# Sparse attention and two dense layers on one core: attention laid out as five-step jobs in issue order, weight conversion cut into three parts

## The chip, the cores and the metric

One NeuronCore of a Trainium2 chip runs the whole program in one launch. The metric is the device time in microseconds (us) of an execution; less is better. Engines by their names in the profile: PE is the matrix engine (TensorE), PEld its weight loads, DVE the vector engine, ACT the scalar engine, POOL the GpSimd engine, SP the queue that issues DMA transfers.

## The reference, cut to what matters

```
scores = (q @ k.T) / 8                     # 4 batches x 8 heads, 576 tokens, head size 64
scores = where(scores >= max(scores) - tau, scores, -1e9)
attn   = exp(scores - max) / (sum + 1e-9)
x  = (attn @ v), heads side by side         # 2304 tokens x 512
h  = x @ w_in;    x = moe_act(h) @ w_out    # 512 -> 2048 -> 512, (h+1)^2/4 between -1 and 1
h  = x @ w_in2;   y = (h * clip(h+3, 0, 6) / 6) @ w_out2
```

## The kernel before

**Attention** is 16 jobs, each one batch and a pair of heads; a job is five blocks of query rows (four of 128, and the last 64 rows of both heads together). So there are 80 steps, and step t stands for block t % 5 of job t // 5. For a step, `em_scores` makes the scores of two heads by eight PE records into two pairs of PSUM banks (P0, P1), DVE negates them into `p` and takes the row extreme `nm` (line 296), ACT takes the exponential `e` (line 300), DVE adds tau into `th` (line 303) and masks, multiplies and sums (line 306). The result `p` is then turned (transposed on PE, line 244): four 128-column pieces a head by `em_pt`, which ACT copies to `Gf` (line 327), and the last 64 columns of both heads by `em_tail`, which ACT copies to `Gt` (line 341). `pv_chunk` multiplies by v (line 361). Once a job `unit_q` and `unit_k` turn the next q and k, `pre_norm` and `em_norm` divide by the sums and write to memory (`xd`).

**Weights** of the dense layers come as 64-bit words; each 128x512 tile (an item) is converted into a pair hi, lo: two ACT operations (lines 111 and 114), a clamp (POOL line 115 during the attention), two DVE operations (lines 122 and 128), a POOL add (line 130), hi (POOL line 133, or ACT line 135 once dense work has begun), lo (POOL line 137). `split_a` and `split_b` are the two halves; 20 items are needed by the first dense pass.

**The first dense pass** (`dense1`: `em_h`, line 485, and `em_part`, line 542; 256 tokens at a time, the first 10 of 16 tiles of the hidden layer) begins when the first batch (four jobs) is done and is laid between the pieces of the attention by a credit: each `yield` of the attention adds `share`, and three matmuls of 128x256 (here called a unit) take 0.33. There are 480 units in all. What is left of it, and the rest of the dense layers, follows the attention.

**Order.** A scheduler with a simulated timeline sets the order of the instructions on each engine, except where `after(...)` puts one instruction behind another on the same engine (`pe_pins`).

Of the kernel before, what the change touches and what calls it, by code (L numbers as in the profile page):

```python
# [18 lines left out]
def kernel(  # L19
# [13 lines left out]
    V, S, G, T = nc.vector, nc.scalar, nc.gpsimd, nc.tensor  # L33
# [52 lines left out]
    def load_w(kind, m, f):  # L86
        t = stage.tile([128, 512, 2], U32, tag="w_raw", name="w_raw", bufs=RAW)
        if kind == "i":
            src = w_bits[m][0][:, f * 256:(f + 1) * 256].rearrange("(k p) n -> p k n", p=128)
            nc.sync.dma_start(out=t.rearrange("p (k n) r -> p k (n r)", k=KD), in_=src)  # L90
        else:
            src = w_bits[m][1][f * 128:(f + 1) * 128, :]
            nc.sync.dma_start(out=t.rearrange("p n r -> p (n r)"), in_=src)
        wraw[kind, m, f] = t

    def after(ins, prev):
        if prev is not None:
            tc.add_manual_dep(ins.ins, prev.ins.name, mybir.DependencyInfo(
                mybir.DependencyClass.NoSync, mybir.DependencyReason.DATA), reason="pace")

    pe_pins = []
    pins = {"S": None, "V": None, "G": None}

    def split_a(kind, m, f):
# [7 lines left out]
        after(x, pins["S"])  # L112
        if mode["att"]:
            S.activation(out=f32(c), in_=f32(t[:, :, 1]), func=ACTF.Abs)
            G.tensor_scalar(
                out=f32(c), in0=f32(c), scalar1=122879.9921875, scalar2=2.0 ** -15, op0=ALU.min, op1=ALU.max)
        else:
            S.activation(out=f32(c), in_=f32(t[:, :, 1]), func=ACTF.Abs)
            x = V.tensor_scalar(
                out=f32(c), in0=f32(c), scalar1=2.0 ** -15, scalar2=122879.9921875, op0=ALU.max, op1=ALU.min)  # L120
            after(x, pins["V"])
        V.tensor_scalar(out=c, in0=c, scalar1=3, scalar2=0x3FFFFFFF,  # L122
                        op0=ALU.logical_shift_left, op1=ALU.bitwise_and)
        wc[kind, m, f] = (hi, lo, c, t, r)

    def split_b(kind, m, f):
        hi, lo, c, t, r = wc.pop((kind, m, f))
# [3 lines left out]
        after(x, pins["G"])  # L131
        if mode["att"] and not mode["mlp"]:
# [10 lines left out]
    class Weights:  # L143


        def __init__(self):
# [3 lines left out]
            self.mid = False  # L150
# [9 lines left out]
        def half(self):  # L160
            if self.done < len(self.items):
                it = self.items[self.done]
                if not self.mid:
                    self.prefetch()
                    split_a(*it)
                else:
                    split_b(*it)
                    self.done += 1
                    self.prefetch()
                self.mid = not self.mid  # L170

        def one(self):
            n = self.done
            while self.done == n and n < len(self.items):
                self.half()

        def upto(self, n):
            while self.done < min(n, len(self.items)):
                self.half()
# [20 lines left out]
    mode = {"mlp": False, "att": True, "step": False, "t": 0, "s": 0, "n": 0}  # L200
# [4 lines left out]
    qt, kt = {}, {}  # L205
# [4 lines left out]
    def load_q(j):  # L210
# [3 lines left out]
        for h in HEADS:  # L214
            src = q[b, 2 * hp + h]
            nc.sync.dma_start(out=qn[:, 0:4, h * D:(h + 1) * D], in_=rows(src))
            nc.sync.dma_start(out=qn[0:TAIL, 4, h * D:(h + 1) * D], in_=src[MAIN:SEQ, :])

    def load_k(j):
# [3 lines left out]
        for h in HEADS:  # L223
            src = k[b, 2 * hp + h]
            nc.sync.dma_start(out=kn[:, 0:4, h * D:(h + 1) * D], in_=rows(src))
            for r in range(2):
                nc.sync.dma_start(out=kn[r * TAIL:(r + 1) * TAIL, 4, h * D:(h + 1) * D], in_=src[MAIN:SEQ, :])

    def load_v(j):
# [4 lines left out]
        for h in HEADS:  # L234
            src = v[b, 2 * hp + h]
            nc.sync.dma_start(out=t[:, 0:4, h, :], in_=rows(src))
            nc.sync.dma_start(out=t[h * TAIL:(h + 1) * TAIL, 4, h, :], in_=src[MAIN:SEQ, :])
# [5 lines left out]
    def turn(out, in_, pin):  # L243
        x = T.transpose(out, in_, ident)  # L244
        if pin:
            pe_pins.append(x)

    def unit_q(j):
# [3 lines left out]
        for c in range(5):  # L252
            turn(tm[:, c * 128:(c + 1) * 128], qn[:, c, :], c == 0)
        load_q(j + 1)
# [3 lines left out]
    def unit_k(j):  # L258
# [4 lines left out]
        for i, c in enumerate((4, 0, 1, 2, 3, 4)):  # L263
            turn(tm[:, i * 128:(i + 1) * 128], kn[:, c, :], i == 0)
        load_k(j + 1)
# [5 lines left out]
    def em_scores(j, i):  # L271

        last = i == NBLK - 1
# [4 lines left out]
        prev = None  # L278
        c = slice(i * 128, i * 128 + (TAIL if last else 128))
        for x, (h, e) in enumerate(((0, 0), (1, 1), (0, 1), (1, 0)) if last else ((0, 0), (1, 0), (0, 1), (1, 1))):  # L280
# [541 lines left out]
```

## Time and profile before

| | |
|---|---|
| median of three runs | 1201.52 us (1201.37 to 1201.78) |
| the profiled execution | 1200.08 us, of which 1198.3 us from the first to the last instruction (the span) |
| PE / DVE / ACT / POOL busy in the span | 1138.7 / 579.6 / 627.5 / 418.8 us |

PE is called busy from the start of a matmul to its modelled end, and matmuls overlap, so that a busy PE is not one at its peak. The stages are read from a table of stretches (rows below) and not from these totals.

### The profile page before, as it was taken

The page shows a single profiled execution, that of the slowest core. Times are in us where ns is not written, and L with a number is a line of the kernel's source. Part 1 is how long each engine was busy: PE and PEld are TensorE (multiplying, and loading weights), DVE is VectorE, ACT ScalarE, POOL GpSimd, SP SyncE. Part 2 cuts the span into 40 slices and gives each one's busy share as a digit, 9 for nine tenths or more (in the row PEclk, how much of TensorE's full clock was granted, in tenths as well). Part 3 has the DMA queues.
Part 4 walks back from the last instruction along what each step waited for, and adds up shares of the span by engine and source line. Part 5 has one row for each costly group of instructions (what it writes and reads, how often), then busy time and mean ns, then how long its engine had stood idle before and what let it go on. Part 6 is the DMA issues. An engine that isn't in the chain of part 4 may idle for free.

```text
span 1198.3 us, 17942 instructions
## 1 busy us (share of the span) xinstructions
PE 1138.7 (95%) x6656; PEld 906.7 (76%) x6656; DVE 579.6 (48%) x1196; ACT 627.5 (52%) x1217; POOL 418.8 (35%) x397
## 2 busy tenths in 40 slices
PE   4877799998999999999999999999999999999998
PEld 3444477876777787777888988888888888888886
DVE  3899865456555565553652575555740121121111
ACT  4667766565665665664665676654542222233222
POOL 1767531110111111112673666656742213222221
PEclk9999889999999999999999999999999999999999
DMA  4444421212111222003431244453210010010000
GB/s 114 117 133 135 128 81 30 51 50 59 54 35 31 59 59 68 21 20 107 149 103 47 81 136 150 152 168 98 88 43 15 1 58 9 1 44 2 18 1 35
DMA packets 106791, 82.43 MB, mean 69 GB/s; under 512 B 66512, under 2 KB 90576, under 8 KB 106704
## 3 DMA queue, kind: packets, MB, share of 16 engines
q1 hardware_dynamic: 106704, 81.29, 23.0%
q8 instruction: 52, 0.85, 0.3%
q14 instruction: 35, 0.29, 0.1%
HBM read 63.96 MB, written 17.30 MB: 68 GB/s over the span
## 4 chain that ended last, share of the span: by engine, by line
PE 83%; DVE 6%; ACT 4%; DMA 3%; SPq 2%; issue 2%; POOL 0%; ACTq 0%; DVEq 0%
PE Q L485 33%; PE P L527 26%; PE Q L542 7%; PE Q L361 6%; PE P L284 5%; PE Q L244 5%; DVE p L306 2%; DVE p L296 2%; DMA w_raw<-in_moe_w_in_dram 1%; PE P L244 1%; ACT e L300 1%; DMA w_raw<-in_moe_w_out_dram 1%; DVE w_c L122 1%; ACT r L494 1%; DVE w_c L128 1%
## 5 line engine op out<-in xcount | busy, mean ns | idle before, releaser
L503 POOL TENSOR_TENSOR gl<-r,gh 128x512 fp32r<-128x512 f32 (+1 forms) x190 | 205.9, 1084 | 641.7 <-ACT gh L502 624.1
L485 PE MATMUL Q<-xh,wih 128*128 128x512 f32 (+1 forms) x760 | 264.5, 349 | 0.7 <-ACT xh L468 0.5
L485 PE MATMUL Q<-xl,wih 128*128 128x512 f32 (+1 forms) x760 | 257.8, 339 | 0.2 <-DVE xl L469 0.2
L485 PE MATMUL Q<-xh,wil 128*128 128x512 f32 (+1 forms) x760 | 257.6, 339 | 0.0
L499 DVE SCALAR_TENSOR_TENSOR r<-r,Q 128x512 f32<-128x512 f32 (+1 forms) x80 | 50.7, 633 | 248.9 <-ACT r L498 248.8
L485 PEld LDWEIGHTS Q<-xh,wih 128*128 128x128 f32 x760 | 144.7, 191 | 29.9 <-issue 10.6
L502 ACT ACTIVATE gh<-r 128x512 fp32r<-128x512 f32 (+1 forms) x190 | 99.9, 526 | 121.5 <-PE P L527 53.3
L485 PEld LDWEIGHTS Q<-xl,wih 128*128 128x128 f32 x760 | 144.8, 191 | 16.5 <-DVE xl L469 0.7
L485 PEld LDWEIGHTS Q<-xh,wil 128*128 128x128 f32 x760 | 144.6, 190 | 15.6 <-issue 0.5
L296 DVE TENSOR_SCALAR_CACHE_REDUCE p<-P 128x576 f32<-128x576 f32 x144 | 104.1, 753 | 80.0 <-PE Q L244 71.5
L306 DVE SCALAR_TENSOR_TENSOR p<-p,th,e 128x576 f32<-128x576 f32 x144 | 130.9, 923 | 24.0 <-ACT e L300 17.4
L244 PE MATMUL Q<-ident,p 128*128 128x128 f32 (+1 forms) x656 | 113.8, 287 | 21.1 <-DVE p L306 10.1
L300 ACT ACTIVATE e<-p,nm 128x576 f32<-128x576 f32 x144 | 109.8, 773 | 32.7 <-DVE p L296 31.6
L498 ACT ACTIVATE r<-Q,three 128x512 f32<-128x512 f32 (+1 forms) x80 | 51.4, 643 | 143.4 <-PE Q L485 140.3
L244 PEld LDWEIGHTS Q<-ident,p 128*128 128x128 f32 (+1 forms) x656 | 74.6, 143 | 63.0 <-DVE p L306 11.7
L284 PE MATMUL P<-kt,qt 64*128 64x288 f32 (+1 forms) x640 | 109.1, 450 | 13.7 <-DVE p L296 7.5
L496 DVE SCALAR_TENSOR_TENSOR r<-r,Q 128x256 f32<-128x256 f32 (+1 forms) x110 | 55.0, 500 | 131.9 <-ACT r L495 129.5
L527 PE MATMUL P<-woh,gh 128*128 128x512 f32 x288 | 111.9, 390 | 0.6 <-DVE ob L580 0.6
L527 PE MATMUL P<-wol,gh 128*128 128x512 f32 x288 | 112.2, 390 | 0.0
L527 PE MATMUL P<-woh,gl 128*128 128x512 f32 x288 | 110.9, 390 | 0.0
L130 POOL TENSOR_TENSOR w_c<-w_c,w_raw 128x512 int32<-128x512 int32 x64 | 87.4, 1366 | 39.3 <-DVE w_c L128 28.1
L327 ACT ACTIVATE Gf<-Q 128x512 f32<-128x512 f32 x128 | 75.0, 591 | 48.6 <-PE Q L244 48.5
(81 smaller groups left out, 1865.2 us busy)
## 6 DMA issues: line engine op xcount, KB each, us to landing
w_raw<-in_moe_w_in_dram SPq DMA_DIRECT2D x32, 512.0 KB, 3.8
w_raw<-in_moe_w_out_dram SPq DMA_DIRECT2D x32, 512.0 KB, 3.6
xst<-xd SPq DMA_DIRECT2D x28, 256.0 KB, 3.2
kn<-in_k_dram SPq DMA_DIRECT2D x32, 128.0 KB, 2.6
qn<-in_q_dram SPq DMA_DIRECT2D x32, 128.0 KB, 2.6
vn<-in_v_dram SPq DMA_DIRECT2D x32, 128.0 KB, 2.6
xd<-xu SPq DMA_DIRECT2D x16, 256.0 KB, 2.5
x2d<-ob SPq DMA_DIRECT2D x16, 256.0 KB, 3.4
```

The costliest lines, as they stand in the source:

```text
L130: x = G.tensor_tensor(out=c.bitcast(I32), in0=c.bitcast(I32), in1=r, op=ALU.add)
L244: x = T.transpose(out, in_, ident)
L284: mm = T.matmul(o, qt[j][r, c], kt[j][r, k0:k0 + HS], start=True, stop=True, skip_group_check=True)
L296: V.tensor_scalar(out=p[:, x], in0=s[:, :, 0:HS], scalar1=-1.0, scalar2=3e38, op0=ALU.mult, op1=ALU.min, accum_out=nm[:, x:x + 1])
L300: S.activation(out=e, in_=p[:, x], func=ACTF.Exp, bias=nm[:, x:x + 1], scale=-1.0)
L306: V.scalar_tensor_tensor(out=p[:, x], in0=p[:, x], scalar=th[:, x:x + 1], in1=e, op0=ALU.is_le, op1=ALU.mult, accum_out=zt[j][:, z:z + 1])
L327: S.activation(out=f[:, h, :, d0:d0 + 128], in_=tm.rearrange("p (c n) -> p c n", c=4), func=ACTF.Copy)
L485: mm = T.matmul(h, l[:, kk * 128:(kk + 1) * 128], r, start=(x == 0), stop=(x == 3 * KD - 1))
L502: x = S.activation(out=gh, in_=r, func=ACTF.Copy)
L503: y = G.tensor_tensor(out=gl, in0=r, in1=f32(gh), op=ALU.subtract)
L527: T.matmul(a, l, r, start=(first and x == 0), stop=(last and x == 2))
L542: mm = T.matmul(o, l, r, start=(f == 0 and x == 0 and i == 0), stop=(f == NF1 - 1 and x == 2 and i == 1), skip_group_check=True)
```

## The change: what it does

- `Chain` wraps all five engines. While the attention runs, each instruction is put behind the one that was issued before it on its engine, so that the order there is the order of the code.
- A step is written as five pieces, with a place for dense work after each: (1) scores of t, the turned tail of t-2 in spare columns of a score bank, the row extremes, the exponentials of t, the masks of t-1; (2) the first turned half of t-2, and q or k of the next job; (3) normalization; (4) a part of the product with v of the job before; (5) the second turned half of t-2. Before, turns stood one step behind the scores (the tail two).
- `th` goes from DVE to POOL, the copy of the tail from ACT to DVE.
- A weight item is converted in three parts. Before dense work begins, one part a step (before: one half a step, and one more every third step); from then on two parts a step, and what `ahead1` demands at once.
- The credit is 0.22 a piece until the 20 items are converted, then 0.53 (before: 0.57).
- q, k and v of later jobs are loaded a step later (`later`), x for the dense pass earlier (`load_x`), tau first of all.

```diff
+    class Chain:
+        def __getattr__(self, name):
+            fn = getattr(self.engine, name)
+            def issue(*a, **k):
+                x = fn(*a, **k)
+                if mode["att"]:
+                    after(x, self.last)
+                    self.last = x
+                return x
+            return issue
+    V, S, G, T, Q = (Chain(e) for e in (nc.vector, nc.scalar, nc.gpsimd, nc.tensor, nc.sync))
...
+                (split_1, split_2, split_3)[self.stage](*it)
+                self.stage = (self.stage + 1) % 3
...
-        tl = bank("Q0" if mode["mlp"] else "Q3")
-            S.activation(out=t[:, d0:d0 + 128], in_=tl[:, 0:128], func=ACTF.Copy)
+        tl = s[:, 1, 320:448]
+            V.tensor_copy(out=gt_[:, d0:d0 + 128], in_=tl)
...
-        V.tensor_scalar(out=th[:, 0:n], in0=nm[:, 0:n], scalar1=taus[:, 0:1], scalar2=None, op0=ALU.add)
+        G.tensor_scalar(out=th[:, 0:n], in0=nm[:, 0:n], scalar1=taus[:, 0:1], scalar2=None, op0=ALU.add)
...
+        for t in range(n + NBLK):
             mode["t"] += 1
             mode["step"] = True
+            j, i = divmod(t, NBLK)
+            due, later[:] = later[:], []
+            ss = em_scores(t) if t < n else [unit_bank()]
+            if 0 <= t - 2 < n:
+                em_tail(t - 2, ss[-1])
+            if t < n:
+                em_first(t, ss)
+            if 0 <= t - 2 < n:
+                em_tail_copy(t - 2, ss[-1])
+            if t < n:
+                em_exp(t)
+            if 0 <= t - 1 < n:
+                em_mask(t - 1)
             yield
+            copy = em_pt(t - 2, 0) if 0 <= t - 2 < n else None
+            if i == 1:
+                unit_q(j + 1)
+            if i == 2:
+                unit_k(j + 1)
+            if copy:
+                copy()
+            yield
+            if i == 1 and j:
                 pre_norm(j - 1)
+            if i == 4 and j:
                 em_norm(j - 1)
                 done_jobs.add(j - 1)
+            yield
+            if j and i < 4:
+                em_pv(j - 1, "aabb"[i], ((0, 1, 2), (3, 4))[i % 2])
+            yield
+            if 0 <= t - 2 < n and order[t - 2][1] < NBLK - 1:
+                em_pt(t - 2, 1)()
+            for fn, x in due:
+                fn(x)
+            yield
...
+                if (g, 0) not in loaded_x:
+                    load_x(g)
+                    for _ in range(8 if mode["att"] else 0):
+                        yield None
...
-            if mode["t"] >= 3 and mode["step"]:
+            if mode["t"] >= 4 and mode["step"]:
                 mode["step"] = False
-                weights.half()
-                if mode["t"] % 3 == 0:
-                    weights.half()
+                weights.third()
...
-        credit = min(credit + share, 3.0)
+        piece += 1
+        if piece % 5 in (0, 2) and weights.done < 2 * NF1:
+            weights.third()
+        credit = min(credit + shares[weights.done == 2 * NF1], 3.0)
```

In the rows of order below, those of the changed kernel all carry line 44, the line in `Chain` that issues them. First DVE before dense work begins, before the change, at the second job (a number behind `P` is one of the score buffers):

```order
L296 TENSOR_SCALAR p,nm<-P_481 128x576
L296 TENSOR_SCALAR p,nm<-P_482 128x576
L122 TENSOR_SCALAR w_c<-w_c 128x512
L303 TENSOR_SCALAR th<-nm,taus 128x2
L128 SCALAR_TENSOR_TENSOR w_c<-w_raw,w_c 128x512
L306 SCALAR_TENSOR_TENSOR p,z<-p,th,e 128x576
```

The same engine and place in the changed kernel:

```order
L44 TENSOR_SCALAR p,nm<-P_429 128x576
L44 TENSOR_SCALAR p,nm<-P_430 128x576
L44 COPY Gt<-P_430 128x128
L44 SCALAR_TENSOR_TENSOR p,z<-p,th,e 128x576 x2
L44 TENSOR_SCALAR w_c<-w_c 128x512
L44 SCALAR_TENSOR_TENSOR w_c<-w_raw,w_c 128x512
```

The masks (`p,z<-p,th,e`) that stand behind the row extremes of a step are now those of the step before, `th` has left the engine, the tail copy has come, and the two weight operations stand behind the masks, once in three steps.

Second, ACT of the changed kernel in step 36, where dense work and conversion run side by side and `ahead1` demands two items at once:

```order
L44 ACTIVATE e<-p,nm 128x576
L44 ACTIVATE Gf<-Q_2035 128x4x128
L44 ACTIVATE w_raw<-w_raw 128x512
L44 ACTIVATE w_c<-w_raw 128x512
L44 ACTIVATE woh_2041<-w_c 128x512
L44 ACTIVATE w_raw<-w_raw 128x512
L44 ACTIVATE w_c<-w_raw 128x512
L44 ACTIVATE woh_2068<-w_c 128x512
L44 ACTIVATE Gf<-Q_2085 128x4x128
```

Each `woh` needs the POOL add of its own item, which comes after the second row above it; the second `Gf` copy of the attention stands behind both. Before, these rows stood apart, as here during the second job:

```order
L111 ACTIVATE w_raw<-w_raw 128x512
L300 ACTIVATE e<-p,nm 128x576
L327 ACTIVATE Gf<-Q_464 128x4x128
L300 ACTIVATE e<-p,nm 128x576
L114 ACTIVATE w_c<-w_raw 128x512
L367 ACTIVATE xu<-Q_455 128x320
```

Third, PE of the changed kernel late in the attention, from the end of a step's product with v into the next step:

```order
L44 MATMUL Q_5127<-xh,wil_552 128x256
L44 MATMUL Q_5155<-ident,p 128x128 x4
L44 MATMUL Q_5071<-gh,woh_1757 128x256
L44 MATMUL Q_5071<-gl,woh_1757 128x256
L44 MATMUL Q_5071<-gh,wol_1758 128x256
L44 MATMUL P_5164<-kt,qt 128x288
L44 MATMUL P_5165<-kt,qt 128x288
L44 MATMUL P_5164<-kt,qt 128x288
L44 MATMUL P_5165<-kt,qt 128x288
L44 MATMUL P_5165<-ident,p 128x128
```

The first row ends a tile of the hidden layer (`em_h`); the next rows are the second turned half, one unit of `em_part`, the scores and the tail. From step 40 on, every step holds eight units, and the end of `em_h` stands in its fourth or fifth piece, right ahead of or behind that turned half. By the order, the changed kernel has laid 0 units ahead of the scores of step 26, 54 ahead of step 40 and 368 ahead of step 79.

## Rows read from the trace of the kernel before

**Rows 1.** Busy time by stretches (us from the span's start).

```profile
core 0: us, PE busy (x) PEld busy (x) DVE busy (x) ACT busy (x) POOL busy (x), PEclk, DMA share, GB/s
33.40:146.30 112.90, 86.63 (x545) 51.72 (x543) 101.93 (x219) 78.43 (x156) 74.97 (x73) 0.92 0.45 126
296.00:536.00 240.00, 236.67 (x1768) 182.71 (x1766) 135.38 (x372) 148.24 (x319) 33.47 (x49) 1.00 0.16 44
700.00:1198.30 498.30, 493.45 (x2275) 411.52 (x2273) 162.66 (x226) 195.15 (x329) 192.13 (x153) 1.00 0.19 59
```

**Rows 2.** Timeline of PE: scores of step 3, q in steps 3 and 23, scores of step 79.

```profile
22.40 1.24 PE L284 MATMUL P<-kt,qt 64*128 64x288 f32 x8 [0.53 <-DVE p L296]
33.37 0.76 PE L244 MATMUL P<-ident,qn 128*128 128x128 f32 x5
146.29 0.77 PE L244 MATMUL P<-ident,qn 128*128 128x128 f32 x5
529.71 1.19 PE L284 MATMUL P<-kt,qt 64*64 64x288 f32 x8
```

**Rows 3.** Timeline of DVE: the first weight item; `pre_norm` in steps 45 and 80.

```profile
26.36 0.43 DVE L122 TENSOR_SCALAR w_c<-w_c 128x512 uint32<-128x512 uint32 x1 [3.75 <-POOL w_c L115]
295.86 0.57 DVE L378 TENSOR_SCALAR z<-z 128x9 f32<-128x9 f32 x1
535.90 0.17 DVE L378 TENSOR_SCALAR z<-z 128x9 f32<-128x9 f32 x1
```

**Rows 4.** Groups of instructions in 33.4 to 146.3 us: busy, mean ns | idle before.

```profile
L306 DVE SCALAR_TENSOR_TENSOR p<-p,th,e 128x576 f32<-128x576 f32 x36 | 42.2, 1188 | 6.7 <-ACT e L300 5.6
L128 DVE SCALAR_TENSOR_TENSOR w_c<-w_raw,w_c 128x512 uint32<-128x512 uint32 x18 | 12.6, 702 | 0.2
L122 DVE TENSOR_SCALAR w_c<-w_c 128x512 uint32<-128x512 uint32 x17 | 12.5, 733 | 1.2 <-POOL w_c L115 1.2
L303 DVE TENSOR_SCALAR th<-nm,taus 128x2 f32<-128x2 f32 x15 | 5.6, 371 | 0.3
L341 ACT ACTIVATE Gt<-Q 128x128 f32<-128x128 f32 x16 | 4.4, 274 | 0.0
L111 ACT ACTIVATE w_raw<-w_raw 128x512 int32<-128x512 uint32 x18 | 12.3, 682 | 12.8 <-DMA w_raw<-in_moe_w_in_dram 8.9 <-DMA w_raw<-in_moe_w_out_dram 3.9
L130 POOL TENSOR_TENSOR w_c<-w_c,w_raw 128x512 int32<-128x512 int32 x17 | 23.6, 1390 | 24.0 <-DVE w_c L128 21.5 <-DVE z L378 2.5
L115 POOL TENSOR_SCALAR w_c<-w_c 128x512 f32<-128x512 f32 x18 | 13.1, 728 | 8.4 <-ACT w_c L114 7.5
```

**Rows 5.** Groups of instructions in 296 to 536 us.

```profile
L485 PE MATMUL Q<-xh,wih 128*128 128x256 f32 x140 | 44.3, 316 | 0.2 <-DVE r L496 0.2
L542 PE MATMUL Q<-gh,woh 128*128 128x256 f32 x132 | 41.8, 317 | 0.0
L306 DVE SCALAR_TENSOR_TENSOR p<-p,th,e 128x576 f32<-128x576 f32 x63 | 51.5, 832 | 8.8 <-ACT e L300 5.3
L496 DVE SCALAR_TENSOR_TENSOR r<-r,Q 128x256 f32<-128x256 f32 x34 | 14.2, 418 | 25.5 <-ACT r L495 25.2
```

**Rows 6.** Timeline of PE: the first and the last of nine dense matmuls in a row.

```profile
226.78 0.28 PE L542 MATMUL Q<-gh,woh 128*128 128x256 f32 x1
...
227.73 0.28 PE L542 MATMUL Q<-gh,wol 128*128 128x256 f32 x1
```

**Rows 7.** Longest wait of PEld in 296 to 536 us: us, times, longest.

```profile
PEld Q L485 <- issue: 6.9, 16, 0.5
```

**Rows 8.** PE groups of the first pass: two rows before 529.7 us, two in 554 to 600 us.

```profile
L485 PE MATMUL Q<-xh,wih 128*128 128x256 f32 x220 | 70.1, 319 | 0.2 <-DVE r L496 0.2
L542 PE MATMUL Q<-gh,woh 128*128 128x256 f32 x195 | 62.1, 318 | 0.1
...
L542 PE MATMUL Q<-gh,woh 128*128 128x256 f32 x27 | 7.7, 285 | 0.1
L485 PE MATMUL Q<-xh,wih 128*128 128x256 f32 x4 | 1.1, 283 | 0.0
```

More of the change, by code (lines that the diff above doesn't have):

```diff
@@ L149, in __init__ @@
             self.done = 0
[L150 removed]
+            self.stage = 0
         def add(self, m, fs):
@@ L158, in prefetch, with third, half @@
                 self.loaded += 1
-        def half(self):
+        def third(self):
             if self.done < len(self.items):
                 it = self.items[self.done]
-                if not self.mid:
+                if self.stage == 0:
                     self.prefetch()
-                    split_a(*it)
-                else:
-                    split_b(*it)
+                (split_1, split_2, split_3)[self.stage](*it)
+                self.stage = (self.stage + 1) % 3
+                if self.stage == 0:
                     self.done += 1
                     self.prefetch()
[L170 to L175, printed above, removed]
+        def half(self):
+            if self.stage == 0:
+                self.third()
+                self.third()
+            else:
+                while self.stage and self.done < len(self.items):
+                    self.third()
         def upto(self, n):
             while self.done < min(n, len(self.items)):
-                self.half()
+                self.third()
     weights = Weights()
@@ L353, in pv_chunk, with em_pv @@
+        return copy
+    o_t = {}
+    def em_pv(j, g, cs):
         n, d0 = GROUPS[g]
         f, t = gt[g, j]
-        if c == 0:
-            if j not in xu:
-                xu[j] = ap.tile([128, SEQ], F32, tag="xu", name="xu", bufs=2)
-            o_t[j, g] = bank("Q1")
-        o = o_t[j, g][:, 0:n]
-        for h in HEADS:
-            mm = T.matmul(o[h * D:(h + 1) * D], vn[j % 2][:, c, h, :], f[:, h, c] if c < 4 else t,
-                          start=(c == 0), stop=(c == 4), skip_group_check=True)
-            after(mm, pe_pins[-1] if h == 0 else prev)
-            prev = mm
@@ L365, in pv_chunk @@
-        if c == 4:
-            del gt[g, j], o_t[j, g]
-            S.activation(out=xu[j][:, d0:d0 + n], in_=o, func=ACTF.Copy)
-    def pv_run(n):
-        for _ in range(min(n, len(pvq))):
-            pv_chunk()
+        for c in cs:
+            if c == 0:
+                if j not in xu:
+                    xu[j] = ap.tile([128, SEQ], F32, tag="xu", name="xu", bufs=2)
+                o_t[j, g] = bank("Q1")
+            o = o_t[j, g][:, 0:n]
+            for h in HEADS:
+                T.matmul(o[h * D:(h + 1) * D], vn[j % 2][:, c, h, :], f[:, h, c] if c < 4 else t,
+                         start=(c == 0), stop=(c == 4), skip_group_check=True)
+            if c == 4:
+                del gt[g, j], o_t[j, g]
+                S.activation(out=xu[j][:, d0:d0 + n], in_=o, func=ACTF.Copy)
@@ L386, in em_norm @@
     def em_norm(j):
-        while any(x[0] == j for x in pvq):
-            pv_chunk()
-        load_v(j + 2)
+        later.append((load_v, j + 2))
         b, hp = jobs[j]
```

242 lines of the change are left out of this document (113 added, 129 removed).

## The prediction

> **What bounds the kernel now.** I read the stretches first, then the timeline of each engine inside them. From 700 us to the end PE is busy 493.5 of 498.3 us at a granted clock of 1.00 [rows 1]: nothing in the attention can change that part but by starting it earlier. So the question is when the first dense pass is done.
>
> Before dense work begins, DVE is the tightest engine: from the q of step 3 to that of step 23 [rows 2], 20 steps take 112.9 us, 5.65 us a step, and DVE is busy for 101.9 of them, 5.1 us a step, PE for 86.6 [rows 1]. In that stretch the masks take 1188 ns each, against 832 ns later [rows 4, 5]; POOL is busy for 66% of the first and 14% of the second [rows 1]. So POOL's weight work seems to cost DVE some 0.36 us a mask. An early stall adds to it: the first item's clamp was late and DVE stood 3.75 us in front of line 122 [rows 3], so that q came at 33.4 us although the scores of the same step had begun at 22.4 [rows 2].
>
> With dense work mixed in, PE is the bound. From step 45 to step 80 (295.9 to 535.9 us [rows 3]) 35 steps take 240 us, 6.86 us each, PE called busy for 236.7 [rows 1]. Nine dense matmuls stand 0.95 us apart, first to last [rows 6], so one costs 0.119 us and a unit 0.356. The stretch holds 140 + 132 units [rows 5], 7.8 a step or 2.77 us. The attention's share of PE with all its gaps is then 6.86 - 2.77 = 4.1 us a step. Those gaps are mostly not waits for another engine: the longest in sum is "issue" [rows 7], time in which nothing that the profile shows was waited for, as where PE goes from 64-row or 64-column tiles to whole ones and back.
>
> **The change part by part.** I divide the new run by the steps that the order shows, and price each stretch.
>
> *To step 25, attention alone.* One part a step is a third of an item, where 18 items in 20 steps [rows 4] were 0.9. DVE loses 0.57 items' worth of lines 122 and 128 (0.57 x 1.43 = 0.8 us a step) and `th` (5.6 / 20 = 0.3). POOL keeps a third of an item: the clamp 0.73, the add 1.39, and hi and lo, which I estimate at 2.2 together from those two, so 4.3 / 3 = 1.4 us, and takes `th`. For `th` on POOL no row exists; the nearest is the clamp, 728 ns for 128x512 [rows 4], so between nothing and 0.7 us, and I take 0.3, as 128x2 is smaller. With 0.2 for the normalization this is 1.9 us of a step of 4.5, 43% in place of 66%, so a mask's stretch of 0.36 falls to 0.23 us and 1.8 masks a step save 0.2. The tail copy is new on DVE: ACT took 274 ns for it [rows 4], so I take 0.25 (0.2 to 0.4). Sum for DVE: 5.1 - 0.8 - 0.3 - 0.2 + 0.25 = 4.05 us. PE needs its 4.1. Two engines that hand a step to and fro and need the same time can't be full both; the masks, now a step late, no longer wait for their own exponentials, so most of the 0.55 us that DVE idled goes. I take 4.5 us a step (4.1 if they mesh, 5.6 if nothing of it works).
>
> The first weight item now stands behind the exponentials of step 3, and its loads are issued ahead of that; the 3.75 us should be hidden. The scores of step 3 began at 22.4 us [rows 2]; two turned inputs move ahead of them, so I take 23. Step 25 begins at 23 + 22 x 4.5 = 122 us, step 26 at 126.5. The q, k and v loads of SP go a step later each, which four more steps before their use hide; the x loads have eight pieces, about 7 us, and cost a few us once if the write before them is slow.
>
> *Steps 26 to 39.* 54 units, 3.9 a step: PE 4.1 + 3.9 x 0.356 = 5.5 us. 13 items are left, 0.93 a step: DVE 4.05 - 0.5 + 1.33, one dense operation of 418 ns [rows 5] in some two of three steps, and 0.2 for POOL's company, 5.4 us. ACT works 148.2 / 35 = 4.2 us a step later on [rows 1], less 0.3 for the tail copy and about 0.5 for fewer units, and with two operations of 0.68 [rows 4] and hi of about as much for each item 5.3 us. Three engines at 5.3 to 5.5 us, each in the order of issue: I add 0.5 for their waiting. Once, two items are demanded inside one step and the rows of ACT show hi standing right behind its own first operations: ACT waits for clamp, two DVE operations and add, 0.73 + 1.43 + 1.39 = 3.6 us, twice, 7 us or 0.5 a step. Together 6.5 us (5.5 to 8). Step 40 begins at 126.5 + 14 x 6.5 = 217.5 us.
>
> *Steps 40 to 78.* 314 units in 39 steps, 8.05 a step, 2.87 us. The end of `em_h` falls behind the step's masks, where DVE is free, and its three ACT operations end before the next exponentials are due; so I see no new wait and take the 4.1 us of before. 6.95 us a step, 271 us: step 79 at 488.5 us. All that stands behind a waiting instruction now waits too: 0.2 us a step would be 8 us.
>
> *The rest.* Before, the scores of step 79 began at 529.7 us with 415 units done [rows 8], and 31 were left at 554 us [rows 8]; in one piece these would end at 565 us. So from step 79 on 35.3 us, of which 65 units take 23.1, 12.2 for the attention's end. After, 112 units are left: 39.9 + 12.2, the end of the first pass at 540.6 us.
>
> *What follows* is 1198.3 - 565 = 633.3 us of a full PE; conversions there are cut in other halves, with the same operations, hidden behind PE as before (DVE busy 162.7 of 498.3 us [rows 1]). Span 540.6 + 633.3 = 1173.9 us. With the 1.8 us around the span, the profiled time goes from 1200.1 to 1175.7, by 24.4 us; from the median of the runs shown, 1201.5, this gives **1177 us**.
>
> **A rule beside the trace.** That a mask takes 1188 ns beside a busy POOL and 832 ns beside an idle one is the rows' own [rows 4, 5]. The Trainium skill (SBUF — State Buffer, "Who interferes with whom") says that a DVE instruction with two SBUF inputs contends with a GpSimd instruction that reads SBUF, and (its section on the two sides) that the loser is held for the whole instruction. By that rule, with every POOL microsecond falling on a mask, the first stretch would cost up to 1.9 - 0.4 = 1.5 us a step more, 33 us, and the kernel would be slower; the mean of the rows, 0.36 us a mask at 66% of POOL, agrees with a lock but with one that is met only part of the time.
>
> **Rivals.**
> - *Better meshing.* 4.1 us in the first stretch (-9) and 5.5 in the second (-14): 1154 us. For it: DVE has idle time to give, and the masks' slack is a whole step. Against: a two-engine loop and one late POOL add stop it. 0.15.
> - *No effect in the first stretch.* Steps stay at 5.6 us, because PE, DVE and ACT wait for each other as before: 22 x 1.1 = 24 us, 1201 us. For it: PE's busy time there is already 86.6 of 112.9 [rows 1]. Against: DVE's work falls by a fifth. Of half of that effect, 1189. 0.12, most of it at the half.
> - *Order of issue stalls the mixed steps* (slower). `em_h` writes one bank, which comes free when DVE has done its product; if ACT has the two exponentials and a copy ahead of it, PE waits about 1 us a step: 39 us, 1216 us. It decides from 24.4 / 39 = 0.63 us a step. For it: PE has no freedom left, where the old order put it around such waits. Against: the place of `em_h`'s end in the shown order. 0.13. The Trainium skill (TensorE: Matmul & The Clock Gate, on the array's architecture) says that ACT and DVE are strict queues; no row here shows the contrary, and it is why such a wait would spread.
> - *The lock of the rule above in full:* 1210 us, 0.05.
>
> **How the numbers follow.** Forecast 0.55, own range 1165 to 1190. A measurement of this kernel tells some 0.2% (2.4 us) from no change. Faster: 0.55 + 0.15 + 0.08 of the second rival = 0.78; same 0.04; slower 0.18. The range drops about half of the first rival and most of the two slow ones: 1158 to 1206.
>
> **What would show it.** Right: steps 3 to 25 at 4.5 us with masks near 1.06 us; step 26 near 127 us, 40 near 218, 79 near 489; PE full from 541 us. Wrong: step 25 later than 135 us (the first term), over 7.5 us a step from 40 on with PE waiting for DVE line 496 or for a copy (the third), or PE waiting for weights after the attention, where I priced nothing.

## The result and the profile after

The changed kernel takes 1217.69 us (median of 4 runs, 1215.38 to 1224.28), the kernel before 1201.44 (4 runs): 1.0144 times as long, 95% interval 1.0105 to 1.0184. It is slower by 1.4%; it was forecast to become faster, at 1177 (1158 to 1206). The profiled execution took 1217.43 us, with a span of 1215.6.

All instructions of the changed kernel stand in one helper, line 44, so its rows are told apart by tile. First the timeline of PE: the scores of steps 3, 25, 26, 40 and 79, which answer to [rows 2]. In the rows, `P` and `Q` are PSUM banks, `Gf` is the copy of a turned half, `xu` the product with v that waits for the normalization, `r` a tile of the hidden layer, `xh` and `xl` the pair into which x is split, and `ob` a finished block of the first dense pass.

```profile
25.91 1.24 PE L44 MATMUL P<-kt,qt 64*128 64x288 f32 x8 [0.78 <-ACT kt L44]
...
130.27 1.24 PE L44 MATMUL P<-kt,qt 64*128 64x288 f32 x8 [2.17 <-DVE xu L44]
...
134.95 1.24 PE L44 MATMUL P<-kt,qt 64*128 64x288 f32 x8
...
247.36 1.24 PE L44 MATMUL P<-kt,qt 64*128 64x288 f32 x8 [1.42 <-DVE xu L44]
...
528.30 1.19 PE L44 MATMUL P<-kt,qt 64*64 64x288 f32 x8
```

The forecast beside them, in us. "Late" is measured less forecast; "added" is how much of that came about since the row above:

| scores of step | forecast | measured | late | added |
|---|---|---|---|---|
| 3 | 23 | 25.9 | 2.9 | 2.9 |
| 25 | 122 | 130.3 | 8.3 | 5.4 |
| 26 | 126.5 | 135.0 | 8.5 | 0.2 |
| 40 | 217.5 | 247.4 | 29.9 | 21.4 |
| 79 | 488.5 | 528.3 | 39.8 | 9.9 |
| end of span | 1173.9 | 1215.6 | 41.7 | 1.9 |

Half of the miss was made in 14 steps. The same stretches by busy time, granted clock (PEclk) and DMA, which answer to [rows 1]:

```profile
core 0: us, PE busy (x) PEld busy (x) DVE busy (x) ACT busy (x) POOL busy (x), PEclk, DMA share, GB/s
25.90:130.30 104.40, 86.53 (x584) 52.78 (x584) 77.43 (x221) 65.94 (x117) 48.78 (x59) 0.95 0.34 91
135.00:247.40 112.40, 84.83 (x547) 60.55 (x546) 65.80 (x174) 69.18 (x133) 57.72 (x65) 0.89 0.33 90
247.40:528.30 280.90, 264.49 (x2006) 207.65 (x2006) 148.41 (x427) 160.39 (x320) 67.51 (x97) 1.00 0.19 50
700.00:1215.60 515.60, 511.30 (x2421) 429.66 (x2419) 169.13 (x243) 208.52 (x359) 202.97 (x164) 1.00 0.19 60
```

In the first stretch DVE is no longer tight, 77.4 of 104.4 us, and PE is not full either. In the second, the 14 mixed steps, no engine is busy for over 76% of the time: they wait for each other. What PE waited for there (us in all, times, longest):

```profile
PE Q L44 <- ACT Gf L44: 16.0, 9, 7.3
PE Q L44 <- DVE r L44: 4.1, 4, 1.9
PE P L44 <- DVE xu L44: 3.8, 3, 1.8
PE Q L44 <- ACT xh L44: 2.5, 1, 2.5
PE Q L44 <- DVE xl L44: 0.7, 1, 0.7
PE P L44 <- DVE p L44: 0.5, 1, 0.5
```

These six make 27.6 us, all the time that PE was not busy in the stretch. ACT, in the same stretch, waited 17.3 us for POOL's add of a weight item:

```profile
ACT woh L44 <- POOL w_c L44: 12.5, 4, 3.7
...
ACT wih L44 <- POOL w_c L44: 4.8, 2, 3.1
```

PE's waits in the third stretch, 247.4 to 528.3 us (16.4 us not busy, where the kernel before had 3.3 in 240 us [rows 1]):

```profile
PE Q L44 <- ACT ob L44: 6.9, 4, 2.2
PE Q L44 <- DVE ob L44: 6.0, 4, 1.7
PE Q L44 <- DVE xl L44: 1.8, 4, 0.6
PE P L44 <- DVE xu L44: 1.4, 1, 1.4
...
PE Q L44 <- DVE r L44: 0.3, 1, 0.3
```

**Two places read closely.** At the end of the second job (timeline of PE, the same job's earlier steps ahead of it for comparison):

```profile
67.10 1.83 PE L44 MATMUL Q<-Gf,vn 128*64 128x320 f32 x12
...
69.58 1.24 PE L44 MATMUL P<-kt,qt 64*128 64x288 f32 x8
...
78.89 2.29 PE L44 MATMUL P<-kt,qt 64*128 64x288 f32 x8 [2.76 <-DVE xu L44]
...
82.37 2.83 PE L44 MATMUL Q<-Gf,vn 128*64 128x256 f32 x12
```

The next job's scores need the bank in which the turned norm stands, and DVE reads it behind two masks (timeline of DVE):

```profile
75.83 1.20 DVE L44 SCALAR_TENSOR_TENSOR p<-p,th,e 128x576 f32<-128x576 f32 x1
...
76.97 0.81 DVE L44 SCALAR_TENSOR_TENSOR p<-p,th,e 128x576 f32<-128x576 f32 x1
...
77.70 1.04 DVE L44 TENSOR_TENSOR xu<-xu,P 128x512 f32<-128x512 f32 x3
```

PE stood for 2.76 us and then worked at the lower of its two levels, 1.2 GHz; by stretches:

```profile
62.00:75.50 13.50, 12.16 (x87) 7.24 (x87) 11.12 (x29) 9.15 (x18) 6.72 (x9) 1.00 0.35 86
78.90:85.10 6.20, 6.20 (x25) 3.41 (x25) 2.48 (x7) 3.04 (x5) 1.39 (x3) 0.50 0.42 122
```

So 6.2 us of work took twice as long as at the upper level: the wait cost nearly 3 us, and the clock behind it 3 more.

The longest wait of the mixed stretch is the one that the shown order of ACT held, two `woh` with a copy behind them; counted from 0, as the steps are here, it stands in step 34 and not 36. PE, then ACT, then POOL:

```profile
204.17 0.60 PE L44 MATMUL Q<-ident,p 128*128 128x128 f32 x4
...
214.47 1.12 PE L44 MATMUL Q<-ident,p 128*128 128x128 f32 x4 [7.26 <-ACT Gf L44]
...
208.14 0.63 ACT L44 ACTIVATE woh<-w_c 128x512 fp32r<-128x512 f32 x1 [3.29 <-POOL w_c L44]
...
213.30 0.63 ACT L44 ACTIVATE woh<-w_c 128x512 fp32r<-128x512 f32 x1 [3.43 <-POOL w_c L44]
213.83 0.58 ACT L44 ACTIVATE Gf<-Q 128x512 f32<-128x512 f32 x1
...
206.83 1.28 POOL L44 TENSOR_TENSOR w_c<-w_c,w_raw 128x512 int32<-128x512 int32 x1 [1.28 <-DVE w_c L44]
...
211.98 1.28 POOL L44 TENSOR_TENSOR w_c<-w_c,w_raw 128x512 int32<-128x512 int32 x1 [1.27 <-DVE w_c L44]
```

ACT idled 6.7 us (3.29 and 3.43) with a copy behind that the attention needed: PE had made the input of that copy by 204.8 us, the copy began at 213.83, and PE stood for 7.26 us until it was done. That ACT is a strict queue, as the Trainium skill has it (TensorE: Matmul & The Clock Gate, on the array's architecture), is what these rows show too.

### The profile page after: what moved, and what is told of

Its sections match the earlier page's. It is cut to its first block, busy times and chain, and to the rows that moved or that the text cites. A ratio compares the mean times of both kernels' runs of the same rounds, so it can differ in the third digit from the quotient of the medians.

```text
span 1215.6 us, 17845 instructions
## 1 busy us (share of the span) xinstructions
PE 1131.6 (93%) x6656; PEld 907.5 (75%) x6656; DVE 551.8 (45%) x1212; ACT 608.6 (50%) x1128; POOL 459.9 (38%) x470
## 5 line engine op out<-in xcount | busy, mean ns | idle before, releaser
L44 POOL TENSOR_TENSOR gl<-r,gh 128x512 fp32r<-128x512 f32 (+1 forms) x190 | 201.6, 1062 | 541.3 <-ACT gh L44 520.2
L44 DVE SCALAR_TENSOR_TENSOR r<-r,Q 128x512 f32<-128x512 f32 (+1 forms) x190 | 105.7, 557 | 473.5 <-ACT r L44 472.0
L44 PE MATMUL Q<-xh,wih 128*128 128x512 f32 (+1 forms) x760 | 268.2, 353 | 10.4 <-DVE r L44 5.7
L44 ACT ACTIVATE e<-p,nm 128x576 f32<-128x576 f32 x144 | 105.5, 774 | 91.3 <-DVE p L44 91.3
L44 PE MATMUL P<-kt,qt 64*128 64x288 f32 (+1 forms) x640 | 104.4, 447 | 22.0 <-DVE xu L44 14.1
L44 DVE SCALAR_TENSOR_TENSOR p<-p,th,e 128x576 f32<-128x576 f32 x144 | 115.7, 836 | 0.6
L44 PE MATMUL Q<-ident,p 128*128 128x128 f32 x576 | 90.6, 282 | 17.1 <-ACT Gf L44 16.7
L44 ACT ACTIVATE Gf<-Q 128x512 f32<-128x512 f32 (+1 forms) x160 | 84.4, 544 | 38.0 <-PE Q L44 37.9
L44 POOL TENSOR_SCALAR th<-nm,taus 128x2 f32<-128x2 f32 (+1 forms) x80 | 58.3, 729 | 103.1 <-DVE p L44 92.0
L44 PEld LDWEIGHTS P<-kt,qt 64*128 64x128 f32 (+1 forms) x640 | 55.2, 184 | 46.7 <-issue 17.6
```

The source lines that it names most:

```text
L44: x = fn(*a, **k)
```

## The experiments

Each is an edit to the changed kernel. The table has the median and, from the starts of scores in its one profile, us a step in three stretches of steps; the medians of the kernel before beside them were 1199.9 to 1200.9. The expectations name the mixed stretch at 7.5 or 8.3 us where they count from the turns of q (steps 26 to 41) or from DVE's first p; from scores to scores it is 8.03.

| run | us | 6 to 21 | 26 to 40 | 40 to 79 |
|---|---|---|---|---|
| changed kernel | 1217.7 | 5.00 | 8.03 | 7.20 |
| e1 | 1220.1 | 4.97 | 7.77 | 7.33 |
| e2 | 1230.2 | 5.07 | 8.07 | 7.41 |
| e3 | 1252.1 | | | |
| e4 | 1234.5 | 4.99 | 8.26 | 7.61 |
| e5 | 1224.9 | 4.46 | 7.36 | 7.57 |
| e6 | 1248.9 | 6.57 | 8.38 | 7.41 |
| e7 | 1220.9 | 5.26 | 8.25 | 7.33 |
| e8 | 1218.3 | 4.46 | 8.06 | 7.40 |
| e9 | 1215.7 | 4.99 | 7.86 | 7.19 |
| e10 | 1207.4 | 4.46 | 7.58 | 7.24 |
| e11 | 1229.7 | 5.04 | 8.37 | 7.10 |
| e12 | 1234.4 | 5.10 | 8.21 | 7.69 |
| e13 | 1240.1 | 4.46 | 8.52 | 7.91 |
| e14 | 1237.9 | 4.46 | 8.48 | 7.85 |
| e15 | 1221.8 | 5.10 | 8.25 | 7.20 |
| e16 | 1215.5 | 4.46 | 8.36 | 7.21 |
| e17 | 1250.4 | 4.99 | 8.07 | 7.91 |
| e18 | 1196.9 | 5.10 | 6.72 | 7.15 |

Two cautions. Runs whose edit leaves the first stretch alone have 4.99 to 5.10 us there, so 0.1 us a step tells nothing. And the column of the mixed stretch is not like with like everywhere: by the PE rows, 54 units of dense work lie ahead of step 40 in most runs, but 67 in e4, e12, e13 and e14, 89 in e7, 120 in e6, 58 in e5 and 52 in e17, and a unit was priced at 0.356 us.

The measured time lies in a range named beforehand in e9, e10 and e11 (there the rival's), within 2 us of the rival's range in e1, e7, e8, e15 and e16, and outside of every named range in the others (e14, whose second range is counted from e13, came 2.2 us below it).

### The first stretch

**e1.**
```diff
-        if not last:
-            mode["s"] += 1
         ss = [unit_bank() for _ in range(1 if last else 2)]
```


> One line of the changed kernel undone: the count of score banks is no longer stepped once more ahead of a block's two banks, so the first head's scores go to the bank that was used longest ago and not to the one that a turned q, k or norm has just used. Theory A, first part (the scores wait for the bank's reader, which stands behind other work in the order of issue): between 38 and 113 us PE waits 8.2 us for DVE xu and 2.3 + 3.7 us for ACT qt, 14.2 us of 75; over the 108 us of the attention-only stretch that would be 20 us, of which I expect half, 10 us, and 1 us a job in the 3 mixed ones before step 40: 1205 us (1200 to 1210), with steps 6 to 21 at 4.5 us. Rival (the other bank has a reader that is as late, the tail copy or the second head's p): 1217 within 3 us, with a wait for DVE p or the tail copy of the same size in place of xu and qt.

Ratio to before 1.0165 (1.0135 to 1.0196), no gain: the first two scores go to the two banks in turn, so both must be free, whichever comes first. PE's wait for xu stayed, 6.0 us between 46 and 112 us (8.2 in the changed kernel).

**e5.**
```diff
+            if i == 4 and j:
+                em_norm(j - 1)
+                done_jobs.add(j - 1)
             if 0 <= t - 1 < n:
                 em_mask(t - 1)
             yield
...
-            if i == 4 and j:
-                em_norm(j - 1)
-                done_jobs.add(j - 1)
```


> One move in the order of issue: in a job's last step the transposes and the three multiplications of the normalization are issued ahead of the masks of the step before, not behind them. Theory D: in the changed kernel PE stands 2.8 us before the next job's first scores, because their bank's reader on DVE (xu) stands behind two masks, and then runs at half the clock for some 6 us (the scores 2.29 us in place of 1.24, the values' product 2.83 in place of 1.83), in all 4 to 5 us a job. It expects steps 6 to 21 at 4.4 to 4.6 us in place of 5.0, 10 to 20 us less in all: 1197 to 1207. Rival (DVE's work is only exchanged, the masks now late for the next turns): 1214 to 1220.

1.0207 (1.0184 to 1.023). The cause is right, 4.46 us a step, and the total wrong. Step 25 begins 7.6 us earlier than in the changed kernel and step 40 7.8 us; what was won was lost in steps 40 to 79, 7.57 us each in place of 7.20. Marking the job done two pieces earlier had moved all dense work, which e8 undoes.

**e8.** As e5, but `done_jobs.add` stays where it was.

> The norm ahead of the masks, as in the run before, but the job is marked done where it was, so that the dense work begins at the same piece and its units stand at the same places of the steps as in the changed kernel. Theory D (the wait for xu and the half clock behind it are worth 8 us before dense work, and what that run lost later came from the two pieces by which all dense work had moved): steps 6 to 21 at 4.5 us, steps 40 to 79 at 7.1 as in the changed kernel, 1206 us (1202 to 1210). Rival (the norm's new place itself costs the mixed steps): steps 40 to 79 at 7.5 us again, 1220 to 1226.

1.0145 (1.0119 to 1.0171), the time of the changed kernel. Both expectations missed: the first stretch keeps its gain of 9.5 us, and the steps behind it eat it, 2.4 us by step 40 and 7.8 from there to 79. The scores behind the norm, and the stretches (us, busy, clock):

```profile
75.90 1.24 PE L44 MATMUL P<-kt,qt 64*128 64x288 f32 x8 [0.89 <-DVE xu L44]
```
```profile
25.90:120.70 94.80, 82.26 (x582) 50.55 (x582) 76.81 (x217) 64.21 (x114) 47.99 (x58) 1.00 0.37 100
127.50:240.30 112.80, 87.06 (x547) 61.66 (x546) 62.84 (x169) 68.94 (x133) 55.34 (x64) 0.84 0.33 90
240.30:529.00 288.70, 268.58 (x2006) 210.37 (x2005) 150.34 (x434) 161.18 (x320) 65.03 (x97) 0.98 0.18 48
```

The wait is 0.89 us and the clock stays at 1.00: step 25 begins at 120.7 us, where 122 were forecast. Behind it the clock falls to 0.84 and 0.98 (0.89 and 1.00 in the changed kernel), and step 79 begins at 529.0 after all. At 7.40 us a step there, against e5's 7.57, the place of the dense work was only a part of e5's loss. So moving the norm is shown to speed up the first stretch, and is not a gain for the whole by itself.

### `th` and the order as such

**e2.** `G.tensor_scalar(out=th...` becomes `V.tensor_scalar(out=th...`.

> One part undone: the 80 thresholds th go back from POOL to DVE. Theory B (th on POOL, 729 ns each where 300 were priced, waits for p in POOL's queue and holds up the clamp and add of the weights behind it): POOL loses 58 us, steps 26 to 40 fall from 7.5 to about 7.0 us and the kernel to about 1210 us. Theory A (the waits are those of the conversion's own chain and of the banks): DVE gains some 0.25 us a step that it has room for, 1217 within 3 us.

1.0248 (1.0229 to 1.0267): 12.5 us slower than the changed kernel, so `th` on POOL is a gain here. Most of it lies in steps 40 to 79 (7.41 us), and DVE's load does not explain it:

```profile
250.00:538.90 288.90, 272.61 (x2007) 213.79 (x2007) 151.72 (x464) 160.23 (x320) 37.24 (x58) 0.97 0.18 49
```

DVE is busy for about half of the time, PE's order is the same, and PE stands for 16.3 us where it stood for 16.4; what is longer is PE's own work, 272.6 us in place of 264.5, at a granted clock of 0.97 in place of 1.00. Why the clock fell here and not in the changed kernel stays open.

**e3.**
```diff
                 if mode["att"]:
-                    after(x, self.last)
                     self.last = x
```


> The changed kernel without its rule that an engine's instructions keep the order in which they are issued: the scheduler orders each engine while the attention runs. If the order of issue itself costs the 42 us by which the changed kernel misses the forecast (an engine stands in front of one wait while ready work is behind it), this gives most of it back: 1180 to 1195 us. If the order is not the cost (the waits are true ones of data and banks), it stays at 1217 within 6 us, or is slower, up to 1240, because dense matmuls and later steps are then put ahead of the attention.

1.0425 (1.0402 to 1.0448). **e11** frees ACT alone: `S = nc.scalar`.

> The rule that an engine keeps the order of issue is dropped for ACT alone, where the scheduler may pass a copy ahead of an operation that waits; PE, DVE, POOL and SP as changed. Theory A, second part: PE's 16 us in front of ACT's copies in the mixed stretch go, steps 26 to 40 at 7.3 us, 1203 us (1196 to 1210). Rival (the scheduler puts other operations, of later steps or of the dense work, ahead of the exponentials): 1217 to 1240.

1.0248 (1.0224 to 1.0272). Without the rule, and without the pins that the kernel before had in its place, the scheduler's order is worse. So the fixed order is not a loss against the order that the scheduler makes of this code; other free orders were not tried.

### The mixed stretch

**e4.** `split_1` to `split_3` become a generator of six parts (ACT's two; clamp; DVE's two; add; hi; lo), one part issued a piece, two tiles in turn.

> In the mixed stretch the conversion of a weight tile is issued in six parts, one a piece, with two tiles in turn, so that no operation stands in its engine's order less than two pieces behind the one it needs; same operations, same engines, same number. Theory A, second part (in the order of issue the chain from ACT to POOL to DVE to POOL to ACT blocks the engines: 16 us of ACT waiting for POOL's add, 13.8 of DVE waiting for the clamp, and 16 of PE waiting for copies behind them, in 112 us): steps 26 to 40 fall from 7.5 to 6.5 to 6.9 us, 1206 us (1201 to 1211). Rival (the load of three engines is the bound, not their waiting): 1217 within 3 us.

1.0283 (1.0248 to 1.0317), worse than both expectations. It also lays 67 units ahead of step 40, so that its dense work stands in other places, as in e12 below, and it can't tell what the finer parts alone are worth. **e9.**
```diff
-        if mode["att"] and not mode["mlp"]:
+        if mode["att"]:
             G.tensor_scalar(out=hi, in0=f32(c), scalar1=1.0, scalar2=0.0, op0=ALU.mult, op1=ALU.add)
```


> One operation of the mixed stretch moved: the high part of a converted weight tile is made by POOL, as it is while the attention runs alone, and not by ACT, so that no operation of ACT waits for POOL's add; POOL gets 13 operations of 1.1 us more in a stretch in which it is busy for half the time. Theory A, second part (ACT stood 20.7 us in front of that add, and PE 16 us behind ACT's copies): most of the 16 us goes and with it some of the half clock, steps 26 to 40 at 7.2 to 7.5 us in place of 8.3, 1203 us (1198 to 1208). Rival (PE then waits for another link, weights or DVE's product, as with six parts): 1213 to 1222.

1.013 (1.0109 to 1.0151), 2 us below the changed kernel, within the spread of its runs. **e10** is e8 and e9 together.

> The norm ahead of the masks with the dense start unchanged, and the high part on POOL, together. If both causes are real and apart from each other, the gains add: 1192 us (1186 to 1200), faster than the kernel before. If the mixed steps lose again what the first stretch gained: 1205 to 1220.

1.0061 (1.0039 to 1.0083): 10.3 us less than the changed kernel, the lowest time but for e18, and still above the kernel before. Alone the two edits gave nothing and 2 us: their gains don't add up.

**e6** and **e7** issue more thirds while the attention runs alone:
```diff
-            if mode["t"] >= 4 and mode["step"]:
-                mode["step"] = False
+            sub = 0 if mode["step"] else sub + 1
+            mode["step"] = False
+            if mode["t"] >= 4 and sub in (0, 2, 4):
                 weights.third()
```
(e7: `(0, 2)`)

> The pacing of the conversions undone: three thirds a step (at its first, third and fifth piece) in place of one while the attention runs alone, so that all 20 weight tiles are converted by step 24 and the mixed stretch has none; order of issue and everything else as changed; the dense work then goes at its later share from the start. Theory P (the 12 tiles left over cost the mixed stretch some 2.7 us each, by 8.3 us a step where 1.5 of dense and 4.1 of attention are due): steps 6 to 25 at 5.6 to 5.9 us with POOL nearly full, steps 26 to 79 at 7.1 us, 1180 us (1172 to 1190). Rival (a tile costs the same wherever it stands, since the order of issue makes every engine wait for its chain): steps 6 to 25 at 6.5 us or more, 1200 to 1217.

> As the one tile a step, with two thirds a step (first and third piece): 14 tiles by step 25, 6 left for the mixed stretch. Theory P: steps 6 to 25 at 5.3 us, the mixed stretch with conversions half as long, 1197 us (1190 to 1205). Rival: 1208 to 1220, between the changed kernel and the other pace in proportion.

1.0405 (1.0384 to 1.0425) and 1.0178 (1.0152 to 1.0203). In e6 two thirds of a tile more a step cost 1.57 us, 2.4 us a tile; in e7 a third costs 0.26, 0.8 us a tile. The early stretch has room for some, not for all: e6 reaches step 25 33 us later than the changed kernel. In the mixed stretch of e6 no conversion is left, and it still takes 8.38 us a step, but with 120 units in place of 54:

```profile
169.90:287.20 117.30, 103.68 (x743) 81.61 (x742) 55.27 (x160) 63.06 (x127) 25.31 (x37) 0.94 0.14 37
```

With the units beyond 54 taken off at 0.356 us, an estimate, e6 is at 6.7 us a step and e7, which has about half of the conversions there, at 7.4, against 8.03. So a tile in the mixed stretch costs about 1.5 us, and 6.7 us a step is left without any.

**e12.** `piece % 5 in (0, 2)` becomes `(0, 2, 4)`.

> Against the changed kernel one number: in the mixed stretch a third is issued at three pieces of a step and not at two, a tile a step, so that the dense work never demands a tile that isn't there (in the changed kernel it does three times, in steps 32, 34 and 37, of 1, 4 and 2 thirds in one go right behind a paced one). Theory A, third part: the two longest waits of PE in that stretch, 7.3 us at 207 and 3.4 us at 230, come from the thirds issued in one go (ACT stands twice 3.4 us in front of POOL's add, PE behind ACT's copy), and each is followed by some us at half the clock; steps 26 to 40 at 7.3 to 7.6 us, 1205 us (1200 to 1209). Rival (each tile costs ACT its wait, however it is paced): steps 26 to 40 at 8.0 us or more, 1212 to 1220.

1.0281 (1.0258 to 1.0305). **e13** is e8, e9 and e12 together, **e14** adds three pieces of attention behind the first `split_x`.

> No thirds in one go, the norm ahead of the masks with the dense start unchanged, and the high part on POOL. By the sums of the separate runs: 8 us of the first stretch, and in steps 26 to 40 the bursts and the wait for POOL's add, together 1217 - 8 - 14 = 1195 us (1190 to 1201). If the gains of pacing and of POOL's high part are one and the same: 1199 to 1206.

> The three together, and three pieces of attention between the split of the first x block and the first dense matmuls that need it, so that PE doesn't stand 2.3 to 2.5 us in front of ACT's xh and then run the first units at half the clock: 3 to 5 us less than the three together, 1191 us (1186 to 1198). If the start's wait only moves to another place: as the three together, within 2 us.

Ratios 1.0332 (1.0309 to 1.0354) and 1.0309 (1.0288 to 1.033). All three were far off, by steps 40 to 79 at 7.7 to 7.9 us: the last third is issued in step 37 and no longer in 39, the dense work's share rises with it, 13 more units lie ahead of step 40, and the later ones stand elsewhere in the steps.

**e15** and **e16** hold that place: `shares[piece >= 77]` for `shares[weights.done == 2 * NF1]`, on e12 and on e13.

> A tile a step in the mixed stretch, so that none is issued in one go on demand, but the dense work keeps the piece at which its share rises (piece 77, step 39), so that TensorE's order is that of the changed kernel instruction for instruction. Theory A, third part: PE's 16 us in front of ACT's copies fall to 6, as they did with the other run of this pacing, and nothing moves behind step 40: 1209 us (1204 to 1212), steps 40 to 79 at 7.1 us. Rival (each tile's chain costs its wait whatever the pace): 1215 to 1220.

> The same with the norm ahead of the masks (job marked done where it was) and the high part on POOL. If e13 lost its 33 us against e10 by the dense work's shifted place alone, steps 40 to 79 are at 7.1 us again and the whole is at 1200 us (1194 to 1205). If the three edits hinder each other in the mixed stretch: 1207 to 1215.

1.0179 (1.0164 to 1.0194) and 1.013 (1.0112 to 1.0147). Steps 40 to 79 are back at 7.2 us, so the place was what e12 and e13 lost. The mixed stretch is no better without the bursts (PE's waits in e15):

```profile
PE Q L44 <- ACT Gf L44: 9.4, 7, 3.3
PE Q L44 <- DVE r L44: 8.6, 5, 3.9
PE P L44 <- DVE p L44: 6.1, 2, 3.1
PE Q L44 <- ACT xh L44: 4.0, 1, 4.0
```

PE waits less for ACT's copies of the attention, and more for DVE's `r` and `p` and for `xh`. **e18** takes the chain out: in the mixed stretch `split_1` and `split_2` do nothing, so that the kernel leaves out most of the conversion of 12 tiles, and `split_3` is
```diff
+            G.tensor_scalar(out=hi, in0=f32(t[:, :, 1]), scalar1=1.0, scalar2=0.0, op0=ALU.mult, op1=ALU.add)
+            G.tensor_tensor(out=lo, in0=f32(t[:, :, 1]), in1=f32(hi), op=ALU.subtract)
```


> The last 12 weight tiles, those of the mixed stretch, are not converted: of a tile only POOL's two operations are left (a copy of the raw upper halves as the high part, and the difference), and ACT's three, DVE's two and POOL's clamp and add are left out, so that what dense work computes there is not the reference's. TensorE's order is that of the changed kernel instruction for instruction. If the conversion's chain is what makes steps 26 to 40 take 8.3 us, they fall to 6.0 to 6.5 us (4.3 for the attention as later, 1.5 for 59 units, the rest the dense start), 26 to 32 us less in all: 1185 to 1191 us, the mixed stretch of the forecast. If it is the fixed order of attention and dense work by itself, they stay above 7.5 us: 1206 to 1217.

0.9963 (0.9951 to 0.9976). Its stretches, to be set beside the second and third above:

```profile
136.80:230.80 94.00, 80.74 (x545) 58.08 (x544) 54.51 (x150) 52.45 (x102) 47.30 (x55) 0.93 0.40 112
230.80:509.80 279.00, 264.11 (x2007) 207.88 (x2007) 147.51 (x426) 158.08 (x316) 65.38 (x95) 1.00 0.18 49
```

94.0 us for the 14 steps in place of 112.4, with the same order on PE: the conversions of the 12 tiles cost 18.4 us, 1.5 us a tile, as e6 and e7 have it. PE stands 13.3 us in place of 27.6 and works 80.7 in place of 84.8, and its longest kind of wait, 16.0 us for ACT's `Gf`, is down to

```profile
PE Q L44 <- ACT Gf L44: 3.3, 6, 1.3
```

The run takes the conversions' work away together with their waits, so it does not tell the two apart; and 6.7 us a step, above the 6.0 to 6.5 expected, are left without them.

### The place of the dense work

**e17.** `shares[weights.done == 2 * NF1]` becomes `shares[piece >= 80]`, three pieces later.

> Against the changed kernel one number: the share of dense work rises three pieces later (piece 80 in place of 77), some 3 units fewer, everything before step 39 untouched. Theory E (where the dense units and the ends of their groups fall in the steps decides whether PE's waits there are hidden): steps 40 to 79 at 7.5 to 7.9 us in place of 7.1 with the clock at half in a part of it, 1230 us (1222 to 1245). Rival (the place doesn't matter): 7.1 us, 1217 to 1219.

1.0414 (1.0397 to 1.0431), 33 us above the changed kernel, for three pieces, and above the range that was expected. Steps 40 to 79 by stretch, PE's longest waits in them, and one such wait with the clock behind it:

```profile
248.60:557.20 308.60, 281.29 (x2003) 217.70 (x2003) 147.31 (x425) 159.77 (x319) 61.64 (x96) 0.95 0.16 44
```
```profile
PE Q L44 <- ACT ob L44: 13.2, 4, 3.6
PE Q L44 <- ACT xh L44: 7.6, 4, 2.7
```
```profile
328.29 0.52 PE L44 MATMUL Q<-xh,wih 128*128 128x256 f32 x1 [2.68 <-ACT xh L44]
```
```profile
329.00:336.00 7.00, 6.92 (x31) 5.00 (x33) 1.03 (x4) 1.11 (x3) 0.00 (x0) 0.56 0.00 0
```

Where a group of dense work ends (`ob`, `xh`), PE waits for ACT; in the changed kernel these ends fall so that a wait is 2.2 us at most and the clock stays at 1.00, in e17 up to 3.6 us and 0.95. Of the 27.7 us that steps 40 to 79 take longer, 10.9 are waits (27.3 us in place of 16.4) and 16.8 are PE's own work, 281.3 us in place of 264.5.

## Why the prediction was wrong

**The step that failed** is the second term, *Steps 26 to 39* at 6.5 us: they took 8.03, and this is 21.4 of the 41.7 us. The term took PE's work at 5.5 us a step as the bound, with ACT and DVE just below it, and added 1.0 for waiting: 0.5 for three engines of equal load, and 0.5 for ACT's standing before POOL's add, 7 us, once. The work of ACT and DVE was less than priced (69.2 and 65.8 us in 14 steps, 4.9 and 4.7 a step, where 5.3 and 5.4 were forecast). It was the waits that were mis-sized: PE stood 27.6 us where 14 were allowed, and ACT stood before POOL's add for 17.3 us in six waits, not 7. And no price was put on the clock: PE's work took 84.8 us where 77 were priced, at a granted clock of 0.89. The 13.6 us of standing and the 7.8 of slower work are the 21.4.

e18 shows that the conversions, work and waits together, cost 18.4 us here, where the sum had 7 for them and held their work to be hidden. The other 10 us of the miss are there without any conversion: 94.0 us in e18, where 14 steps of 5.5 and 0.5 make 84. No single link of the chain is the cause: taking one away (e9, e15) moved the wait to another reader. Whether the rest is the fixed order or plainly the load of three engines stays open, as the freer orders (e3, e11) were slower.

None of the signs of being wrong that I had named shows this stretch: step 25 came before 135 us, the steps from 40 on stayed below 7.5 us, and PE waited for no weights after the attention. They stood for the first and third terms and for the end; only the list for being right, with step 40 near 218 us, had the second.

**The first term** was mis-sized by 5.4 us, and by 2.9 at its start. There the scores of step 3 wait 0.78 us for `kt` (first row above), and those of step 2 wait for `qt`, turned ahead of them, and then take 2.29 us, where they took 1.24 before:

```profile
20.63 2.29 PE L44 MATMUL P<-kt,qt 64*128 64x288 f32 x8 [0.83 <-ACT qt L44]
```

The work that the term priced for DVE was there: masks even shorter than the 1.06 us given, as the group of DVE over 25.9 to 130.3 us has it (busy, mean ns),

```profile
L44 DVE SCALAR_TENSOR_TENSOR p<-p,th,e 128x576 f32<-128x576 f32 x41 | 32.8, 833 | 0.2
```

which is 0.36 us less than [rows 4], with POOL busy for 47% (48.8 of 104.4 us), so the lock rival got no support; nor did my own rule that a mask's stretch goes with POOL's share, which had left 0.23 us. What was missing was the bank: the normalization was priced as 0.2 us of POOL's work, and I did not ask what stands ahead of its reader on DVE. With that wait out (e8) steps 6 to 21 take 4.46 us, where 4.5 was forecast.

**The third term**, 6.95, measured 7.20, 9.9 us. The wait that I named for the slow rival, `em_h`'s bank, is 0.3 us in all, but its kind was there at another bank: `ob`, 12.9 us of the 16.4 that PE stood. The rival's time of 1216 us came out by another road, its stall in other steps and at another bank: that the number is near is luck. The term holds only for this place of the dense work (e17, 7.91).

**The rest**, 685.4 us, was right (687.3): nothing waits for weights there.

**`th`** took 729 ns on average and not 300, and this cost nothing that a run shows: with it back on DVE the kernel was slower (e2). The chance of 0.78 for faster came from pricing an engine's load where its waits decided; even e18, with the whole chain away, is only 0.4% below the kernel before.

## What to carry to other kernels

In a program whose engines keep the order of issue, price a mixed stretch by what stands behind each waiting instruction, not by the busiest engine: here no engine was busy for over 76%, and the step was 1.5 us longer than forecast. Turned data that shares a bank with the next block's scores should be read ahead of work that nobody waits for; here this won 9.5 us up to step 25, and later waits took it back (e8). And hold the place and the amount of the other work fixed when one edit is tried: three pieces of shift cost 33 us, more than any cause that was sought.

## What was not expected of the hardware

Two waits of PE cost about as much again in clock: 2.76 us of waiting, then 6.2 us at 0.50; 2.68 us, then 7 us at 0.56. It is not a fixed price: with the same order on PE and the same waits for `ob` (up to 2.2 us) steps 40 to 79 ran at 1.00 in the changed kernel and at 0.97 in e2. And an operation on 128x2 elements took about as long on POOL as one on 128x512 had ([rows 4], 728 ns for the clamp), though spans on POOL are rough (`th` took 288 to 1047 ns); the group of the whole span, its 128x1 form with it:

```profile
L44 POOL TENSOR_SCALAR th<-nm,taus 128x2 f32<-128x2 f32 (+1 forms) x80 | 58.3, 729 | 103.1 <-DVE p L44 92.0 <-PE P L44 5.3 <-PE Q L44 5.3
```
